# A retention block and a gated feed-forward block on one core: w_out rounded behind the silus, the left-out tokens loaded later, and k of three pairs put in rows on the chip

## The chip, the cores and the metric

The kernel runs on one core of one Trainium2 chip. The metric is the device time of one execution in microseconds (us). Each kernel is run several times and the median is taken.

## The reference

Retention: q, k and v have the shape (8, 8, 576, 64), that is batch, heads, tokens, head size. For each head the scores q k^T / 8 are multiplied by gamma^(i-j) for j <= i and by 0 otherwise, and the result by v. The heads are laid side by side into x of 4608 tokens by 512. Feed-forward, with w_gate and w_val (512 x 1536) and w_out (1536 x 512):

```
g = x @ w_gate
silu = g * (1.0 / (1.0 + np.exp(-g)))
val = x @ w_val
return (silu * val @ w_out)
```

All of it is float32.

## The kernel before, in words

**Tiles and stages.** Heads are taken in pairs: pair i is batch i // 4 and heads 2 (i % 4) and 2 (i % 4) + 1; HP is 4, so pairs 0 to 3 are batch 0, and there are 32. The feed-forward works on tiles of tokens: a first one of 512 (stage 0) and four of 1024 (stages 1 to 4). Stages 1 to 4 use fast matrix products with fewer multiplications, whose sums of operands are made by VectorE and POOL and partly kept in DRAM. Stage 0 is done plainly: `up0(f)` (L859) for the twelve column blocks f of 128 multiplies the tile by w_gate into one PSUM bank and by w_val into a second (banks A and B for even f, C and E for odd f), then ScalarE takes the silu of the first into `io` (L874) and VectorE multiplies it with the second (L875). `down0(f)` (L880) multiplies by w_out, over all four banks.

**Rounding.** All weights are rounded before use. They lie in 18 pieces (six of w_gate, six of w_val, six of w_out, each for two blocks f), loaded in the sequence `order` (L361); "position" below is a place in it, and positions 7, 10, 13, 15, 16 and 17 are w_out. Each piece has two halves, j = 2 x position and the next. `split(j)` (L389) is two ScalarE operations (L398, L399) that write one of two slots (j % 2); `rounding(j)` (L408) is two VectorE operations (L415, L416) that read the slot, and then it emits split(j + 1). When the second half of a piece has been split, its raw place is free and a later position is loaded into it by `load_w` (L368): from position 5 on by POOL's queue (L379, L381).

**Retention.** `load(i)` (L255) issues a pair's transfers on SP's queue: for the pairs from 4 on kn and v by tokens (L290), and q and k "by columns" into `qk` (L299), 32 x 18 x 32 elements in each of 4 + 4 DMAs, so that every piece of memory read is 32 floats. VectorE then turns q and k into rows of the head size by its 32 x 32 block transposes (L477, inside `transposes`, L455), into qT and kT. kT exists once. `tick(t)` (L787) runs one step of a pipeline over pairs: PE does the values of pair t-2, the states and scores of pair t-1; then a list of pieces follows on ScalarE and VectorE: the copy of the even states (L569), the scaling of kn by ScalarE (`keys`, L492), the outputs of pair t-2 (L614), masks and states of pair t-1 (L565 to L593), and the transposes of pair t.

**The left-out tokens.** Pairs 0 to 3 leave out their last 64 tokens at first. `end_loads` (L668) loads q, k and v of these with 20 small DMAs on POOL's queue; `end_transposes`, `end_scores`, `end_masks`, `end_own`, `end_earlier` and `end_to_x` (L680 to L711) compute them inside ticks HP + 1 to HP + 3. Their tiles lie in `spare`, in the part of `rest` that later holds rounded w_out.

**The order.** Every engine runs its instructions in the order in which the program emits them. For stage 0 this is the list `plan` (L1521 to L1546): for f from 2 to 11, the roundings up to a position (`round_until`), `up0(f)`, loads, and ticks 4 to 9 behind f = 2 (ahead of up0(3)), 3, 5, 7, 10 and 11. After the plan come `down0` with the sums of w_out (POOL and VectorE, L904, stored by SP, L974), and ticks 10 to 13.

Of the kernel before, what the change touches and what calls it, by code (L numbers as in the profile page):

```python
# [132 lines left out]
def kernel(  # L133
# [32 lines left out]
    nc = tc.nc  # L166

    B, H, S, D = q.shape
# [3 lines left out]
    HP = H // 2  # L172
    L = D
    NC = S // L
    NFULL = S // P
    CW = NFULL * P
    SQ = 32
# [66 lines left out]
    def whole(i):  # L244

        return HP <= i < needed(2) - 2

    def scaled(i):

        return 0 < i < HP  # L250
# [4 lines left out]
    def load(i):  # L255
# [27 lines left out]
        else:  # L283
# [11 lines left out]
            if not whole(i):  # L295
                queue.dma_start(out=t[:, CW : CW + D], in_=v[b, 2 * p : 2 * p + 2, CW:S, :])
            for n, src in enumerate((q, k)):
                for a in range(P // SQ):
                    queue.dma_start(  # L299
                        out=qk[a * SQ : (a + 1) * SQ, n],  # L300
                        in_=src[b, 2 * p + a // 2, :, (a % 2) * SQ : (a % 2 + 1) * SQ].rearrange("(j t) d -> t j d", t=SQ))
# [121 lines left out]
    for m in range(2):  # L423
# [9 lines left out]
             spare[:, CW : CW + NC * D].rearrange("p (c d) -> p c d", d=D))  # L433
    end_states = spare[:, 3136:3392].rearrange("p (n d) -> p n d", d=D)
    end_raw = spare[:, 1536:2048].rearrange("p (n x) -> p n x", n=2)
    end_q, end_k, end_v = [spare[:, 2048 + 256 * n : 2304 + 256 * n].rearrange("p (n d) -> p n d", d=L) for n in range(3)]
    end_at = [o.rearrange("p (n i) -> p n i", i=L) for o in (outer[:, 0, 384:512], outer[:, 1, 256:384])]
# [17 lines left out]
    def transposes(i):  # L455
# [12 lines left out]
        else:  # L468
            if light(i):
# [5 lines left out]
                pieces.append(scale_q)  # L475
            for n, t in enumerate((qT, kT)):
                pieces.append(lambda n=n, t=t: nc.vector.transpose(out=t, in_=qk[:, n].rearrange("p j d -> p (j d)")))  # L477

# [308 lines left out]
    def tick(t, lo=HP, hi=NP, spread=False, then=None):  # L787
        go_on(len(pieces))
        if lo <= t - 2 < hi:
            own_values(t - 2)  # L790
            if t == HP + 3:
                st[t - 2]["own"] = end_own(1)
        if lo <= t - 1 < hi:
            new_states(t - 1)
        if lo <= t - 2 < hi:
            earlier_values(t - 2)
            if t == HP + 3:
                end_own(0)
                end_earlier()
        if lo <= t - 1 < hi:  # L800
            scores(t - 1, t - 2 < lo)
            if t == HP + 2:
                end_scores()
# [18 lines left out]
        else:  # L822
            pieces.extend(new)
            pieces.extend([then] if then else [])
        if t == HP + 2:
            pieces.append(end_masks)
        if t == HP + 3:
            pieces.append(end_to_x)
# [673 lines left out]
    nc.gpsimd.tensor_copy(out=last_near, in_=near[:, even_heads])  # L1502
    end_loads()
    FIRST = needed(1) - 2
# [9 lines left out]
    def round_until(i):  # L1514
        while todo and order.index(i) >= todo[0]:
            m = todo.pop(0)
            plan.extend(lambda j=j: rounding(j, j != 2 * len(order) - 3) for j in (2 * m, 2 * m + 1))
# [3 lines left out]
    for f in range(2, NF):  # L1521
        if f == 3:
            plan.append(lambda: tick(HP, HP, FIRST))
        round_until({4: 12, 6: 13, 8: 14, 9: 15, 10: 16, 11: 17}.get(f, f + 2))
        last_half = plan.pop() if f + 1 == NF else None
        plan.append(lambda f=f: up0(f, range(HP)))
        if last_half:
            plan.append(last_half)
        if f + 2 == NF:
            plan.append(lambda: split(2 * len(order) - 2))  # L1530
        if f + 1 == NF:
            plan.append(lambda: pool_places.extend(wide_places))
            plan.append(negate)
        if f - 1 in tick_at and f < 7:
            plan.append(lambda t=tick_at[f - 1]: next_load(t))
        if f in tick_at and f > 2:
            plan.append(lambda t=tick_at[f]: tick(t, HP, FIRST))
            if tick_at[f] == HP + 1:
                plan.append(end_transposes)
# [97 lines left out]
```

## Time and profile before

| | |
|---|---|
| runs | median 1015.77 us of 3 (1014.49 to 1016.64) |
| the profiled execution | 1012.77 us |
| its span, first to last instruction | 1011.0 us |
| granted clock of TensorE | 1.000 |
| DMA, mean over the span | 192 GB/s, 273932 packets, 212328 of them under 512 B |
| SP's queue (q1) | 249448 packets, 99.49 MB, 40.5% of 16 engines' span |
| POOL's queue (q0) | 4176 packets, 14.03 MB, 4.2% |

A profile row of a group or of the timeline names the line, the engine, the operation, what it writes and reads, and the shape; the timeline has the start, the duration, and in brackets how long the engine had stood idle before it and what released it. PE is TensorE (PEld its weight loads), DVE VectorE, ACT ScalarE, POOL GpSimd, SP SyncE. "issue" is time in which an engine waited for nothing that the profile shows. Busy shares are means over stages with different limits, so a change in stage 0 is read from the timelines there.

Busy us of the engines in stage 0 and around it, with the mean busy share of the DMA engines:

| stretch, us | PE | VectorE | ScalarE | POOL | DMA |
|---|---|---|---|---|---|
| 40 to 60 | 20.00 | 12.79 | 11.62 | 10.51 | 1.13 |
| 60 to 80 | 19.48 | 14.04 | 9.39 | 2.22 | 1.05 |
| 80 to 100 | 20.00 | 16.05 | 9.87 | 2.17 | 1.09 |
| 100 to 120 | 18.70 | 18.49 | 16.59 | 3.73 | 0.93 |
| 120 to 140 | 20.00 | 18.41 | 5.60 | 8.93 | 0.96 |

### The profile page before, as it was taken

Reading aid. Unit: us, or ns where it says so; the run is one execution under the profiler, and the core shown is the slowest. Engines: PE = TensorE matmul, PEld = TensorE weight load, DVE = VectorE, ACT = ScalarE, POOL = GpSimd, SP = SyncE. Lnnn points to the kernel's source line nnn. Section 1 sums busy time; section 2 is a strip of 40 time slices with the busy share of each in tenths; the row PEclk is TensorE's granted clock in tenths of the full one; section 3 lists DMA queues with packets and bytes.
Section 4 is the critical chain, followed back from the end, with each engine's and each line's share of the span. In section 5 each row is a group of like instructions: output and inputs, shape, how many; then the busy total and the mean of one; then the engine's idle time right before and its main releaser. Section 6 shows DMA issues by size and latency. Waiting matters only on the chain.

```text
span 1011.0 us, 21336 instructions
## 1 busy us (share of the span) xinstructions
PE 1002.8 (99%) x8330; PEld 827.7 (82%) x8330; DVE 717.8 (71%) x1210; ACT 285.7 (28%) x636; POOL 576.3 (57%) x611
## 2 busy tenths in 40 slices
PE   8999999999999999999999999999999999999998
PEld 7645455888888888888888888888888888888887
DVE  5568988678886676977777678866575767566745
ACT  4654622122423321133321202233320012232110
POOL 3511358979587228565565157746672586566614
PEclk9999999999999999999999999999999999999999
DMA  9999977888787886957578786434454454445553
GB/s 228 276 252 281 200 216 260 211 239 217 168 211 235 219 197 218 211 156 198 177 187 222 179 196 202 151 137 155 162 173 141 156 188 146 148 153 185 178 163 103
DMA packets 273932, 194.44 MB, mean 192 GB/s; under 512 B 212328, under 2 KB 241896, under 8 KB 273832
## 3 DMA queue, kind: packets, MB, share of 16 engines
q1 hardware_dynamic: 249448, 99.49, 40.5%
q10 hardware_dynamic: 20208, 79.57, 24.2%
q0 software_dynamic: 4176, 14.03, 4.2%
q8 instruction: 66, 1.08, 0.5%
q14 instruction: 34, 0.28, 0.1%
HBM read 154.11 MB, written 38.93 MB: 191 GB/s over the span
## 4 chain that ended last, share of the span: by engine, by line
PE 91%; SPq 3%; DMA 2%; DVE 1%; issue 1%; ACT 1%; ACTq 0%; DVEq 0%
PE bankB L1208 12%; PE bankE L1208 12%; PE bankA L1208 12%; PE bankC L1208 12%; PE bankE L1415 7%; PE bankC L1415 7%; PE bankB L1415 7%; PE bankA L1415 6%; SPq L299 2%; PE outer L1208 2%; PE inner L1208 2%; PE outer L517 2%; PE outer L544 1%; PE inner L558 1%; PE inner L528 1%
## 5 line engine op out<-in xcount | busy, mean ns | idle before, releaser
L1061 POOL TENSOR_TENSOR rest<-rest 128x512 f32<-128x512 f32 (+1 forms) x143 | 150.7, 1065 | 158.1 <-DVE rest L1061 110.3
L1223 POOL TENSOR_TENSOR arena<-rest,io 128x256 f32<-128x256 f32 x168 | 123.8, 749 | 78.7 <-ACT io L1222 78.1
L1222 ACT ACTIVATE io<-rest 128x256 f32<-128x256 f32 x192 | 79.3, 417 | 209.9 <-DVE rest L1061 139.2
L1208 PE MATMUL bankB<-rest,arena 128*128 128x256 f32 x428 | 110.1, 381 | 0.0
L1208 PE MATMUL bankE<-rest,arena 128*128 128x256 f32 x424 | 107.8, 379 | 0.0
L1061 DVE TENSOR_TENSOR rest<-bankC,rest 128x512 f32<-128x512 f32 x112 | 75.8, 684 | 40.4 <-PE bankC L1208 23.3
L1061 DVE TENSOR_TENSOR rest<-bankB,rest 128x512 f32<-128x512 f32 x110 | 74.8, 685 | 41.5 <-PE bankB L1208 30.4
L1208 PE MATMUL bankA<-rest,arena 128*128 128x256 f32 x408 | 104.0, 379 | 0.0
L1061 DVE TENSOR_TENSOR rest<-bankA,rest 128x512 f32<-128x512 f32 x112 | 75.9, 685 | 38.8 <-PE bankA L1208 20.2
L1061 DVE TENSOR_TENSOR rest<-bankE,rest 128x512 f32<-128x512 f32 x116 | 78.5, 686 | 29.2 <-PE bankE L1208 17.1
L1208 PE MATMUL bankC<-rest,arena 128*128 128x256 f32 x368 | 94.2, 380 | 0.0
L1208 PEld LDWEIGHTS bankB<-rest,arena 128*128 128x128 f32 x428 | 80.7, 190 | 11.9 <-DVE rest L1061 0.9
L1208 PEld LDWEIGHTS bankE<-rest,arena 128*128 128x128 f32 x424 | 80.5, 190 | 11.0
L1208 PEld LDWEIGHTS bankA<-rest,arena 128*128 128x128 f32 x408 | 77.5, 190 | 10.6
L1208 PEld LDWEIGHTS bankC<-rest,arena 128*128 128x128 f32 x368 | 69.4, 190 | 10.0 <-DVE rest L1061 0.6
L1061 POOL TENSOR_TENSOR arena<-arena 128x256 f32<-128x256 f32 (+1 forms) x76 | 70.6, 951 | 8.3 <-PE bankC L1208 7.0
L1415 PE MATMUL bankE<-arena 128*128 128x256 f32 x264 | 61.0, 381 | 0.0
L1415 PE MATMUL bankC<-arena 128*128 128x256 f32 x264 | 60.9, 380 | 0.0
L1415 PEld LDWEIGHTS bankE<-arena 128*128 128x128 f32 x264 | 49.8, 190 | 7.0 <-POOL arena L904 0.2
L1415 PEld LDWEIGHTS bankC<-arena 128*128 128x128 f32 x264 | 49.9, 190 | 6.9
L1415 PE MATMUL bankB<-arena 128*128 128x256 f32 x240 | 55.3, 380 | 0.0
L1415 PE MATMUL bankA<-arena 128*128 128x256 f32 x228 | 52.5, 380 | 0.0
(294 smaller groups left out, 1880.1 us busy)
## 6 DMA issues: line engine op xcount, KB each, us to landing
arena<-up ACTq DMA_DIRECT2D x60, 896.0 KB, 4.8
arena<-dn ACTq DMA_DIRECT2D x60, 384.0 KB, 3.4
arena<-dn SPq DMA_DIRECT2D x44, 384.0 KB, 4.4
out_dram<-rest SPq DMA_DIRECT2D x31, 256.0 KB, 3.5
qk<-in_q_dram SPq DMA_DIRECT2D x108, 72.0 KB, 4.1
qk<-in_k_dram SPq DMA_DIRECT2D x108, 72.0 KB, 3.8
dn<-rest SPq DMA_DIRECT2D x26, 256.0 KB, 3.1
up<-arena SPq DMA_DIRECT2D x13, 512.0 KB, 3.4
```

The source lines that it names most:

```text
L299: queue.dma_start(out=qk[a * SQ : (a + 1) * SQ, n], in_=src[b, 2 * p + a // 2, :, (a % 2) * SQ : (a % 2 + 1) * SQ].rearrange("(j t) d -> t ...
L517: m = nc.tensor.matmul(value(i, hl, c), s["v"][rows, at], ret[rows, c % 2 if whole(i) else hl, c // 2], start=start, stop=start, skip_grou ...
L528: nc.tensor.matmul(z[half[hl], r, c], s["kn"][chunk(i, hl, 2 * c + r)], s["v"][rows, at], start=True, stop=True, skip_group_check=True)
L544: nc.tensor.matmul(xr[half[hl]] if c + 1 == NC else value(i, hl, c), state[half[hl], c, :], s["qT"][half[hl], ts(c, L)], start=False, stop ...
L558: nc.tensor.matmul(sc[chunk(i, hl, 2 * c + r)[0], r if whole(i) else hl, c], kT[half[hl], at], qT[half[hl], at], start=True, stop=True, sk ...
L1061: eng.tensor_tensor(out=out, in0=a, in1=b, op=ALU.add if sign > 0 else ALU.subtract)
L1208: m = nc.tensor.matmul(b[:, g * TB : (g + 1) * TB], w[:, g], x, start=(opens and g == 0), stop=True, skip_group_check=True)
L1222: nc.scalar.activation(out=s, in_=src[:, 0:TB], func=AF.Silu)
L1223: (nc.vector if busy and o != 2 and qd + 1 < NQ else nc.gpsimd).tensor_tensor(out=hid[:, qd, 2 * H + h, 2 * T + t], in0=src[:, TB : 2 * TB ...
L1415: nc.tensor.matmul(b[:, m * TB : (m + 1) * TB], lhs[:, qd, ts(m, P)], w[:, qd], start=(opens and qd == 0 and m == 0), stop=(qd == NQ - 1), ...
```

## The change

Four things change; the arithmetic and the reference's output stay the same.

1. For pairs 5, 6 and 7 (`by_token`) k is not loaded by columns any more. At the start of `transposes`, ahead of `keys`, VectorE transposes kn, which is loaded by tokens anyway, in 32 x 32 blocks into the place of `qk` that k had; 16 ScalarE copies of 32 lanes (`rows_of_k`) then put the blocks in rows in kT, as a piece at the place of the former transpose of k.
2. In the plan, the roundings of w_out (positions 7, 10, 13, 15, 16, 17) are emitted behind `up0(f)` and so behind its silu and product, not ahead of them. Positions of w_gate and w_val stay ahead.
3. `end_loads` is emitted after up0(6) and its roundings (behind the load of position 13 in POOL's queue, ahead of positions 14 to 17) and not ahead of the plan. What is done with the left-out tokens moves by two ticks, to ticks HP + 3 to HP + 5.
4. The tiles of the left-out tokens move from `spare` to the 1536 columns from `sum_at` on, which the first sums of w_out by POOL use later.

```diff
+    def by_token(i):
+
+        return HP < i < needed(1) - 6
...
-            for n, src in enumerate((q, k)):
+            for n, src in enumerate((q,) if by_token(i) else (q, k)):
...
-    end_states = spare[:, 3136:3392].rearrange("p (n d) -> p n d", d=D)
-    end_raw = spare[:, 1536:2048].rearrange("p (n x) -> p n x", n=2)
-    end_q, end_k, end_v = [spare[:, 2048 + 256 * n : 2304 + 256 * n].rearrange("p (n d) -> p n d", d=L) for n in range(3)]
+    ends_at = rest[:, sum_at : sum_at + 1536]
+    end_states = ends_at[:, 1280:1536].rearrange("p (n d) -> p n d", d=D)
+    end_raw = ends_at[:, 0:512].rearrange("p (n x) -> p n x", n=2)
+    end_q, end_k, end_v = [ends_at[:, 512 + 256 * n : 768 + 256 * n].rearrange("p (n d) -> p n d", d=L) for n in range(3)]
...
-            for n, t in enumerate((qT, kT)):
-                pieces.append(lambda n=n, t=t: nc.vector.transpose(out=t, in_=qk[:, n].rearrange("p j d -> p (j d)")))
+            flat = [qk[:, n].rearrange("p j d -> p (j d)") for n in range(2)]
+            pieces.append(lambda: nc.vector.transpose(out=qT, in_=flat[0]))
+
+            def rows_of_k():
+
+                blocks = flat[1].rearrange("p (g n t) -> p g n t", n=2, t=SQ)
+                to = kT.rearrange("p (c w t) -> p c w t", w=2, t=SQ)
+                for r in range(2):
+                    for hl in range(2):
+                        cs = slice((hl + r) % 2, NC, 2)
+                        gs = slice(hl * (NC // 2 + (1 - r)), hl * (NC // 2 + (1 - r)) + len(range(NC)[cs]))
+                        for w in range(2):
+                            for n in range(2):
+                                nc.scalar.copy(out=to[(2 * hl + n) * SQ : (2 * hl + n + 1) * SQ, cs, w],
+                                               in_=blocks[(2 * r + w) * SQ : (2 * r + w + 1) * SQ, gs, n])
+
+            if by_token(i):
+                nc.vector.transpose(out=flat[1], in_=kn)
+                pieces.append(rows_of_k)
+            else:
+                pieces.append(lambda: nc.vector.transpose(out=kT, in_=flat[1]))
...
-            if t == HP + 3:
+            if t == HP + 5:
                 end_own(0)
                 end_earlier()
...
-            if t == HP + 2:
+            if t == HP + 4:
                 end_scores()
...
-        if t == HP + 2:
+        if t == HP + 4:
             pieces.append(end_masks)
-        if t == HP + 3:
+        if t == HP + 5:
             pieces.append(end_to_x)
...
-    end_loads()
...
-        round_until({4: 12, 6: 13, 8: 14, 9: 15, 10: 16, 11: 17}.get(f, f + 2))
-        last_half = plan.pop() if f + 1 == NF else None
+        if f < 10:
+            round_until(f + 2)
         plan.append(lambda f=f: up0(f, range(HP)))
-        if last_half:
-            plan.append(last_half)
+        if f in (4, 6) or f > 7:
+            round_until({4: 12, 6: 13}.get(f, f + 6))
         if f + 2 == NF:
             plan.append(lambda: split(2 * len(order) - 2))
+        if f == 6:
+            plan.append(end_loads)
...
-            if tick_at[f] == HP + 1:
+            if tick_at[f] == HP + 3:
                 plan.append(end_transposes)
```

More of the change, by code (lines that the diff above doesn't have):

```diff
@@ L824, in tick @@
             pieces.extend([then] if then else [])
-        if t == HP + 2:
+        if t == HP + 4:
             pieces.append(end_masks)
-        if t == HP + 3:
+        if t == HP + 5:
             pieces.append(end_to_x)
```

## The prediction

> **What bounds the kernel now.** I read the page first, then PE's waits, then the timelines of PE, ScalarE, VectorE and POOL between 37 and 130 us, where every edit lies.
>
> ```profile
> span 1011.0 us, 21336 instructions
> ...
> PE 1002.8 (99%) x8330; PEld 827.7 (82%) x8330; DVE 717.8 (71%) x1210; ACT 285.7 (28%) x636; POOL 576.3 (57%) x611
> ```
>
> PE is busy for all but 8.2 us of the span. Its waits from 40 us to 1000 us, in one row (engine, line, what it waited for, us in total, times, longest):
>
> ```profile
> PE bankA L871 <- ACT io L874: 1.8, 2, 1.3
> ```
>
> So between the start-up and the last store only two waits stop PE, and both are waits for the silu (L874) that empties a bank two f earlier. PE's timeline has them (start, us, last bracket: idle before, and releaser):
>
> ```profile
> 71.47 3.70 PE L871 MATMUL bankA<-rest,arena 128*128 128x512 f32 x8 [0.52 <-ACT io L874]
> ...
> 103.74 3.70 PE L871 MATMUL bankA<-rest,arena 128*128 128x512 f32 x8 [1.30 <-ACT io L874]
> ```
>
> They are up0(6) and up0(10). All other f take 6.97 us (54.46 to 61.43, 61.43 to 68.39, 71.47 to 78.44): no further wait is hidden in them. Why was silu(8) late? ScalarE before it:
>
> ```profile
> 99.52 0.69 ACT L398 ACTIVATE rest<-rest 128x512 f32<-128x512 f32 x1 [8.51 <-issue]
> ...
> 102.54 0.66 ACT L399 ACTIVATE rest<-rest 128x512 int32<-128x512 uint32 x1
> 103.11 0.58 ACT L874 ACTIVATE io<-bankA 128x512 f32<-128x512 f32 x1
> ```
>
> Bank A was full at 92, but three splits (L398, L399) stand ahead of the silu, and the first had to wait for a slot that VectorE empties. VectorE was late itself, by column loads of k (and, at 59.55, of q):
>
> ```profile
> 59.55 0.78 DVE L477 STREAM_TRANSPOSE qT<-qk 128x576 f32<-128x576 f32 x1 [1.66 <-DMA qk<-in_q_dram]
> 65.36 0.78 DVE L477 STREAM_TRANSPOSE kT<-qk 128x576 f32<-128x576 f32 x1 [5.03 <-DMA qk<-in_k_dram]
> ...
> 97.44 0.78 DVE L477 STREAM_TRANSPOSE kT<-qk 128x576 f32<-128x576 f32 x1 [3.01 <-DMA qk<-in_k_dram]
> ```
>
> The chain is: column load, kT, rounding, split, silu, PE. What the change can win in this execution is 0.52 + 1.30 = 1.82 us, 0.18% of 1015.77 us, because nothing else stops PE there and its matmuls are the same ones after.
>
> **The change, part by part.**
> (1) k by columns goes for pairs 5, 6, 7: 12 DMAs of 72 KB leave SP (52.17, 69.08, 85.50: 5.61 + 2.13 + 4.32 = 12.1 us of its queue). VectorE's waits of 5.03 and 3.01 go with them. VectorE's work is unchanged: three transposes of 128x576 (0.73 to 0.78 each) read kn in place of qk, and stand earlier, behind the product of the odd f. The new wait there is for kn: at tick 5 ScalarE scaled kn at 54.88 without waiting, and the transpose would come at 54.05, so at most 0.8 us, on an engine that then waits for q until 59.55 anyway. Of keys, which must follow the transpose, I expect no more than that.
> (2) ScalarE gets 48 copies of 32 lanes with 128 or 160 elements. No row has this shape. Below: 128x64 from PSUM, L641, 0.11 from start to next start; above: 128x288 SBUF to SBUF, L474, 0.95 for two, so 0.48. Nearest: L611, 64x128, 0.53 for two at 133.23, next start 0.44 on, so 0.22 each. 16 x 0.22 = 3.5 us a pair (1.8 to 7.7). They run behind keys, where ScalarE stood idle from 57 to 67.18 (tick 5) and from 91.0 to 99.52 (tick 7). At tick 6 there is no such gap, and they delay splits 19 to 21 by 3.5.
> (3) Silus ahead of the w_out splits. silu(4) had splits 14, 15 and 16 in front, and keeps 14; silu(8) had 26 to 28 and keeps 26. A split is 1.13, so each is 2 x 1.13 = 2.3 earlier, on top of VectorE's earlier start. silu(4): q at 59.5, transpose 0.7, rounding 12 from 60.3, split 14 to 62, silu done by 62.7; PE wants it at 70.95. Covered by 8 us.
> (4) The left-out tokens. End matmuls move from ticks 6 and 7 to ticks 8 and 9: tick 6 took 2.56 on PE, tick 7 3.04, tick 8 2.26, so 0.30 and 0.78 are moved, sum zero, but up0(10) comes 1.08 earlier still, at 102.45 - 0.52 - 1.08 = 100.85. The 20 loads leave POOL's queue at 37 and stand behind the weight load of position 13 (w_out), ahead of 14 to 17. What they took:
>
> ```profile
> 37.10 3.81 POOL L672 DMA_DIRECT2D rest<-in_q_dram  x7
> 44.05 0.65 POOL L672 DMA_DIRECT2D rest<-in_q_dram  x1 [3.15 <-DMA rest<-in_moe_w_gate_dram]
> 44.69 4.33 POOL L672 DMA_DIRECT2D rest<-in_k_dram  x8
> 49.01 2.42 POOL L677 DMA_DIRECT2D rest<-in_v_dram  x4
> 51.39 0.75 POOL L381 DMA_DIRECT2D rest<-in_moe_w_out_dram  x1
> ```
>
> That is 14.3 us, with a wait for a load that stands eight places ahead on the queue. In the new place: tick 6 ends on PE at 70.65; ScalarE runs even and keys (1.2) from 69.8, copies 3.5, splits 19 and 20 (2.4), silu(6) 0.5, split 21 1.2, so 78.6; position 13 is issued to 79.3, the 20 loads to 93.6. **Position 14, w_val for f 10 and 11, is issued at 93.6 and not at 87.17.** Its load took 9.4 us (the seven gate and w_val loads of this queue 8.7 to 9.7): 102.3 to 103.0 (103.3). Split 1.25 and the second half of the rounding 0.75 make the weights ready at 104.3 to 105.0. PE wants them for bank B of up0(10) at 100.85 + 3.43 = 104.3. I take half, 0.35 us of a new wait.
> The transposes of these tokens (k issued by 79.3 + 11.9 = 91.2, with 3.7 to 4.6 to land as it had there) end near 96.5 on VectorE; silu(8) follows 2.4 later at 98.9, wanted at 100.85: covered by 2 us.
> (5) end_masks is now the last of tick 8 on VectorE and end_own the second of tick 9 on PE (117.5 + 0.28 = 117.8). In the old order tick 8's last transpose ended at 119.27, because even waited behind a split for w_out of position 17 (issued 105.13, landed 113.6). Masks end 6.0 after that landing. Position 17 follows split 29, which follows position 14: 102.6 + 2.4 = 105.0; at the 5.9 of position 16 it lands at 110.9 and the masks are 0.9 early, at 8.4 they are 1.6 late. With SP's load of pair 9 over by then (it starts when pair 7's rows are copied, 93, not 108) I take 5.9 and no cost.
> (6) end_raw and the rest lie where the first output sums of POOL go (L904 at 108.14), so POOL starts them after tick 9, near 120.5. It did its second only at 119.06 and then stood 9.03 us for stores from 127.7, which SP began at 132.01 behind loads. SP is 12 us earlier: nothing.
>
> Sum: -1.82 + 0.35 = -1.5. The profiled execution's 1012.77 (span 1011.0 and 1.77 around it) becomes 1011.3; it lies 3.00 under the median of the runs, and I apply the difference there: 1015.77 - 1.5 = **1014.3**.
>
> **The rivals.**
> A, the wait is only exchanged: position 14 or 17 lands at the late end of its rows (9.4 to 9.7; 8.4), PE stands 0.7 to 1.6 at up0(10) or in tick 9. For it: DMA share is 0.95 to 1.16 from 85 to 100. Against: 12 loads fewer. 1014.7 to 1015.6, no change. 0.18.
> B, slower: POOL's 20 issues stretch beside the rounding, which now runs there. At the longest weight issue against the shortest (0.98 to 0.70, factor 1.4) 11.2 us of issues become 15.7; with position 9 landing late (2.3 us on split 18) position 14 is issued at 100.4, its weights come at 111.8, and PE stands 7.5: 1015.77 - 1.8 + 7.5 = 1021.5. It decides from an issue of position 14 at about 96.8 on (1.8 won, 2.0 more for the bound). Against: eight issues at 44.69 took 549 to 552 ns, beside rounding until 45.4. 0.14. The Trainium skill, page "SBUF — State Buffer", section "SBUF: two separate sides", states such a rule: while VectorE runs a two-port operation, GpSimd cannot write the descriptors of its DMAs. By that rule this rival would hold; the 549 to 552 ns speak against it here, though on few instructions.
> C, more than the profile has: the runs' median is 3.00 above the profiled execution. Were half of it waits of the same chain, 1.5 more would go: 1012.8, all of it 1011.3. For it: column loads took 2.8 to 11.1 us to land, so the chain can vary. Against: the profile shows nothing of it. 0.18.
> D, copies at 0.48: 4.2 us more at tick 6, which delays positions 13 and 14 by as much; 2.7 slower than before, 1018.5; at half of that, no change. 0.05.
>
> **How the numbers follow.** Forecast 0.45. A measurement can tell about 0.2%, 2.0 us: faster ends at 1013.7. The runs before spread over 2.15 us, so a third of the forecast (0.15) falls below that line, and 0.30 above. Faster 0.15 + 0.18 (C) = 0.33; same 0.30 + 0.18 (A) + 0.02 (D) = 0.50; slower 0.14 (B) + 0.03 (D) = 0.17. The range takes the forecast, A and the near half of C, and leaves out B, the slow part of D and the far end of C: 1011.6 to 1017.0.
>
> **What would show it.** PE's row of waits for L874 gone between 60 and 110; no VectorE wait for in_k columns before tick 8; position 14 issued near 94 and no PE wait on its weights over 0.7; masks ahead of end_own; POOL's issues still 0.55. The prediction is wrong if up0(10) or tick 9 shows a wait over 1.8, if a ScalarE copy takes 0.4, or if the time moves by more than 1.9 with PE's waits as forecast.

## The result and the profile after

After: median 1020.13 us of 5 runs (1018.75 to 1021.29); before, beside it on the same chip, 1015.48 of 5 (1014.49 to 1016.64). The ratio is 1.0047, with a 95% interval from 1.0024 to 1.0070: slower by 4.65 us. The forecast was 1014.3, its range ended at 1017.0. The profiled execution took 1020.75 us with a span of 1018.8.

PE's timeline of after has both waits of before changed. The wait at up0(6) is gone. In their place PE stops three times (start, us, and in the last bracket the idle time and its releaser; L895 is up0, L541 the values in a tick):

```profile
104.80 3.70 PE L895 MATMUL bankA<-rest,arena 128*128 128x512 f32 x8 [3.25 <-ACT io L898]
110.20 3.70 PE L895 MATMUL bankB<-rest,arena 128*128 128x512 f32 x8 [1.71 <-DVE arena L420]
...
124.87 0.46 PE L541 MATMUL outer<-ret,v 64*64 64x64 f32 x16 [1.41 <-DVE rest L717]
```

The first two are up0(10), its gate bank and its second bank; the third is tick 9, which waits for the masks of the left-out tokens. 3.25 + 1.71 + 1.41 = 6.37, against 0.52 + 1.30 = 1.82 in before: 4.55 more, which is the size of the loss in the medians. The two profiled executions themselves lie 7.98 us apart (1020.75 and 1012.77): 4.9 of it in stage 0, 2.3 behind it and 0.7 ahead of it. A second profile of before (below) shows that its own waits differ between executions, so the agreement of 4.55 with 4.65 is partly luck.

What made the first two begins on POOL; where the third comes from is worked out at step 5 below. POOL's timeline from position 13's load to position 14's (L385 and L383 are weights, L696 and L701 the tokens):

```profile
84.94 0.70 POOL L385 DMA_DIRECT2D rest<-in_moe_w_out_dram  x1 [1.99 <-ACT rest L403]
85.64 3.87 POOL L696 DMA_DIRECT2D rest<-in_q_dram  x7
94.50 0.55 POOL L696 DMA_DIRECT2D rest<-in_q_dram  x1 [4.98 <-DMA rest<-in_moe_w_out_dram]
95.03 4.33 POOL L696 DMA_DIRECT2D rest<-in_k_dram  x8
99.36 2.40 POOL L701 DMA_DIRECT2D rest<-in_v_dram  x4
101.72 0.80 POOL L383 DMA_DIRECT2D rest<-in_moe_w_val_dram  x1
```

The form is that of before, 4.33 us for eight issues included. But the eighth token load waits 4.98 us (3.15 in before) for the weight load eight places ahead, and position 14 is issued at 101.72 (the prediction had 93.6). The same two loads, positions 13 and 14, in before's POOL timeline:

```profile
84.39 0.70 POOL L381 DMA_DIRECT2D rest<-in_moe_w_out_dram  x1 [6.66 <-ACT rest L399]
87.17 0.76 POOL L379 DMA_DIRECT2D rest<-in_moe_w_val_dram  x1 [2.07 <-ACT rest L399]
```

Position 13 is issued as late as in before (84.94 against 84.39); the 20 loads behind it put position 14 back by 14.55 us.

ScalarE's timeline shows both ends of the chain, the copies (L494) and what waits (L402 is the first half of a split, L898 the silu):

```profile
56.45 5.11 ACT L494 COPY kT<-qk 32x160 f32<-32x160 f32 x16
...
71.52 0.67 ACT L402 ACTIVATE rest<-rest 128x512 f32<-128x512 f32 x1 [3.19 <-DMA rest<-in_moe_w_gate_dram]
...
102.86 0.67 ACT L402 ACTIVATE rest<-rest 128x512 f32<-128x512 f32 x1 [3.72 <-issue]
...
104.16 0.58 ACT L898 ACTIVATE io<-bankA 128x512 f32<-128x512 f32 x1
...
108.20 0.66 ACT L402 ACTIVATE rest<-rest 128x512 f32<-128x512 f32 x1 [2.32 <-DMA rest<-in_moe_w_val_dram]
```

A copy takes 5.11 / 16 = 0.32 us. The split at 102.86, ahead of silu(8), waits for VectorE; the one at 108.20 waits for position 14's load, 6.5 us after its issue. What held VectorE are the transposes of the tokens:

```profile
97.89 0.45 DVE L706 STREAM_TRANSPOSE rest<-rest 128x256 f32<-128x256 f32 x1 [1.18 <-DMA rest<-in_q_dram]
101.92 0.45 DVE L706 STREAM_TRANSPOSE rest<-rest 128x256 f32<-128x256 f32 x1 [3.58 <-DMA rest<-in_v_dram]
```

The second one reads k, whose eight loads POOL issued until 99.36. The row names a load of v, the last of its queue; in the kernel the instruction reads only k.

### The profile page after: what moved, and what is told of

It is laid out like the page before. It is cut to its first block, busy times and chain, and to the rows that moved or that the text cites. A ratio compares the mean times of both kernels' runs of the same rounds, so it can differ in the third digit from the quotient of the medians.

```text
span 1018.8 us, 21372 instructions
## 1 busy us (share of the span) xinstructions
PE 1005.5 (99%) x8330; PEld 828.2 (81%) x8330; DVE 718.8 (71%) x1210; ACT 300.5 (29%) x684; POOL 576.4 (57%) x611
## 4 chain that ended last, share of the span: by engine, by line
PE 85%; DMA 3%; POOL 2%; issue 1%; DVE 1%; SPq 1%; ACT 0%; DVEq 0%; ACTq 0%; POOLq 0%
PE bankB L1232 12%; PE bankE L1232 11%; PE bankA L1232 11%; PE bankC L1232 11%; PE bankE L1439 7%; PE bankC L1439 7%; PE bankB L1439 7%; PE bankA L1439 6%; PE inner L1232 2%; PE outer L1232 2%; PE outer L541 2%; DMA rest<-in_moe_w_out_dram 2%; PE outer L568 1%; PE inner L582 1%; PE inner L552 1%; PE bankA L906 1%
```

## The experiments

In all tables "stage 0" is the time from the start of up0(2) to the first down product in the profiled execution, and the waits are those of PE between them. Part 2 is the silus ahead of the w_out roundings, part 1 is k by tokens, parts 3 and 4 are the late loads with their tiles. Each ratio is the one on record, taken against runs of before on the same chip; it is not the quotient of the two medians. A kernel that starts from after is compared with after by these ratios.

### The parts one by one and in pairs

Parts were undone in the changed kernel. Part 1 undone loads k by columns for every pair:

```diff
-        return HP < i < needed(1) - 6
+        return False
```

Part 2 undone has the plan of before:

```diff
-        if f < 10:
-            round_until(f + 2)
+        round_until({4: 12, 6: 13, 8: 14, 9: 15, 10: 16, 11: 17}.get(f, f + 2))
+        last_half = plan.pop() if f + 1 == NF else None
         plan.append(lambda f=f: up0(f, range(HP)))
-        if f in (4, 6) or f > 7:
-            round_until({4: 12, 6: 13}.get(f, f + 6))
+        if last_half:
+            plan.append(last_half)
```

Parts 3 and 4 undone have the loads ahead of the plan, the work on the tokens in ticks HP + 1 to HP + 3 and the tiles in `spare` (of this edit only the plan is shown):

```diff
+    end_loads()
...
-        if f == 6:
-            plan.append(end_loads)
...
-            if tick_at[f] == HP + 3:
+            if tick_at[f] == HP + 1:
                 plan.append(end_transposes)
```

| parts in the kernel | median us | ratio to before, 95% | stage 0 | PE's waits in stage 0 |
|---|---|---|---|---|
| none (before) | 1014.14 | 1.0008 [0.9992, 1.0024] | 86.46 | up0(6) 1.67, up0(10) 1.91 |
| 2 | 1014.36 | 0.9997 [0.9982, 1.0012] | 81.11 | tick 10 1.07 |
| 1 | 1016.58 | 1.0016 [0.9996, 1.0036] | 81.70 | tick 10 1.57 |
| 1, 2 | 1017.45 | 1.0025 [1.0006, 1.0043] | 82.60 | tick 9 1.49, tick 10 0.35 + 1.58 |
| 3, 4 | 1023.19 | 1.0084 [1.0062, 1.0106] | 90.32 | up0(10) 6.63 |
| 2, 3, 4 | 1021.04 | 1.0062 [1.0040, 1.0085] | 88.80 | up0(10) 1.10 + 3.94, tick 9 0.83 |
| 1, 3, 4 | 1024.21 | 1.0104 [1.0083, 1.0125] | 91.10 | up0(10) 8.53 |
| all (after) | 1020.13 | 1.0047 [1.0024, 1.0070] | 87.87 | up0(10) 3.25 + 1.71, tick 9 1.41 |

The row of before is its second profile; the first one, ahead of the prediction, has a stage 0 of 83.01 with waits of 0.52 and 1.30.

**The late loads are enough for a loss.** The four kernels without them lie within 0.25% of before, the four with them 0.47 to 1.04% over it; alone they cost 0.84%. In three of the four pairs with and without them the intervals are apart. In the fourth they overlap: parts 1 and 2 alone are at 1.0025, all four at 1.0047. Part 2 makes good some of the loss: 1.0104 becomes 1.0047, with the intervals apart; 1.0084 becomes 1.0062, with intervals that overlap. PE's wait in the kernel with parts 3 and 4 alone:

```profile
107.42 6.27 PE L895 MATMUL bankA<-rest,arena 128*128 128x512 f32 x8 [6.63 <-ACT io L898]
```

Before as a kernel of its own. Expected:

> The kernel before, unchanged, profiled a second time beside its own timed runs. It settles how much of a difference of 1 to 3 us between two profiled executions is only the execution. In the one profile so far, the stretch from the start of stage 1 to the last instruction took 838.2 us; in after and four variants 839.4 to 840.9. If that rest is chance of the execution, this profile shows 839 to 841 too, with one or two stops of PE called issue near 276, and a span of 1012 to 1014. If the changes cost something behind stage 0, it shows 838.2 and no such stop. Both expect the waits of 0.52 and 1.30 us for the silus again, and a time ratio of 1.000 within 0.002.

The first branch held for that stretch: from stage 1 to the end it took 1016.6 - 176.45 = 840.2 us, as in the variants, with a stop of 1.00 at 277, so it is no cost of the change. The span was 1016.6 and not 1012 to 1014, because the silu waits are larger in this execution, as its PE timeline shows:

```profile
72.85 3.70 PE L871 MATMUL bankA<-rest,arena 128*128 128x512 f32 x8 [1.67 <-ACT io L874]
105.73 5.40 PE L871 MATMUL bankA<-rest,arena 128*128 128x512 f32 x8 [1.91 <-ACT io L874]
```

Behind the second one PE's granted clock is lower. The rows of the windows give the stretch, its length, PE's busy time and instructions, the granted clock, the DMA share and GB/s:

```profile
105.00:110.00 5.00, 4.27 (x7) 0.69 0.97 263
110.00:115.00 5.00, 5.00 (x43) 0.97 1.16 314
```

1.67 + 1.91 + (5.40 - 3.70) = 5.28 us against 1.82 in the other profile. One profile is one draw: this execution took 1018.36 us, the first one 1012.77, and the median lies between. Of the 5.6 us between the two, 3.5 are in stage 0 and 2.0 behind it.

Part 2 alone:

> The kernel before with part 2 alone: w_out rounded behind the silus. Both theories: silu(8) has one split ahead of it and not three, so it is done 2.3 us earlier than at 103.69, silu(4) likewise; PE's waits of 0.52 and 1.30 go: 1.5 to 2.0 us under the kernel before. If the time stays, those waits were no more than the profiled execution's own.

Missed. Both waits went, PE began the down products 2.00 us earlier (120.39 against 122.39), and the time did not move: PE stopped 1.07 at tick 10.

Part 1 alone:

> The kernel before with part 1 alone: k of pairs 5 to 7 in rows by VectorE's blocks and ScalarE's copies; loads of the left-out tokens and roundings of w_out as before. ScalarE gets 48 copies of 0.32 (5.1 us a pair, as measured in after, not 3.5). Theory (the copies put 5.1 us ahead of the splits at tick 6, and the column loads' lateness at tick 7 is gone; the two about cancel): silu(8) is up to 1.5 earlier or later than in before, its wait 0 to 3 us; time within 1.5 of before. Rival (part 1 alone does what it is for: VectorE is ahead, splits and silus follow): both waits of before gone, time 1.5 to 3 under before. Second rival (the copies alone are a loss): wait for silu(8) above 3, time 2 or more over before.

The rival's mechanism held in the trace (both waits under 0.2), its time did not: 1.57 at tick 10, ratio 1.0016.

Parts 1 and 2, tokens early:

> The changed kernel with parts 3 and 4 undone: the left-out tokens load ahead of the plan and are worked on in ticks 5 to 7, in their old place; silus first and k by tokens stay. Theory (the 20 late loads on POOL's queue cost the time, by three waits of PE of 3.25, 1.71 and 1.41 us): all three go, and the two old ones of 1.82 as well, so 1.0 to 2.0 us under the kernel before. Rival 1 (the 48 ScalarE copies cost it, 5.1 us a pair): still 3 to 5 us over the kernel before. Rival 2 (the loss lies behind stage 0): also still over it, with no wait of PE between 60 and 130 us.

Missed, by about 4 us by the ratio: new waits at ticks 9 and 10 came in place of the others, with a granted clock of 0.67 behind the last (130 to 135). So parts 1 and 2 together cost something without the late loads; what makes these waits was not followed up.

Parts 3 and 4 alone:

> The kernel before with the later loads of the left-out tokens alone (parts 3 and 4 of the change); k of pairs 5 to 7 by columns again, w_out roundings ahead of the products again. Theory (three losses that do not need each other; the late loads on POOL are the largest): the weights of position 14 come late for up0(10) again, 2 to 5 us over before, and as the splits stand ahead of the silu again, the wait for silu(8) is 3 or more. Time 1.5 to 4 us over before. Rival (the loss needs the combination: without the copies and with the roundings in their old places, the loads find room): within 1 us of before. A wait of tick 9 for the masks is expected under 0.5 by the theory, since without part 2 the last splits are not moved.

The direction held, the size was twice what was expected: one wait of 6.63, and a lower clock behind it. The split ahead of silu(8) waited 3.91 us for position 14's load, which was issued at 98.00.

Without part 1:

> The changed kernel with part 1 undone: k of the three pairs by columns again, no copies on ScalarE; silus first and late tokens stay. Theory: the late loads alone still make VectorE and position 14 late, but they start up to 8 us earlier without the copies at ticks 5 and 6, so one or two of the three waits stay, smaller: 0 to 3 us over the kernel before. Rival 1: without the copies the loss is gone, 1 to 2 us under the kernel before.

The copies are not needed for the loss: position 13 is issued as late without them (85.42, up0(2) being 0.56 later in this profile). The size was missed: about 6 us over before where 0 to 3 were expected, and the three waits, 5.87 in all, are hardly smaller than in after.

Without part 2:

> The changed kernel without part 2: w_out rounded ahead of the products as in before, with k by tokens and the late loads kept. Theory (late loads hold up0(10), and without part 2 the silus wait behind more splits): waits at up0(10) of 5 to 7 in one, and then a lower granted clock for about 5 us; no wait over 0.5 at tick 9, since PE comes there later; time 1 to 3 over after, like the late loads alone (1.0084). Rival (part 2 is what costs the 1.41 at tick 9, and the rest is as in after): 5 at up0(10), none at tick 9, time 1 to 1.5 under after.

One wait, as the theory had it, but of 8.53, and nearer 6 than 3 us over after by the ratios.

### Where the late loads hold PE

Each of these starts from the changed kernel.

The 20 loads on SP's queue:

```diff
-                    nc.gpsimd.dma_start(
+                    nc.sync.dma_start(
...
-                nc.gpsimd.dma_start(out=end_v[half[hl ^ x], 2 * x : 2 * x + 2],
+                nc.sync.dma_start(out=end_v[half[hl ^ x], 2 * x : 2 * x + 2],
```

> The changed kernel with the 20 loads of the left-out tokens issued on SP's queue, at the same place of the program, so that positions 14 to 17 have POOL's queue to themselves. Theory: position 14 is issued when its split frees the place (near 87), the wait of 1.71 goes, and the loads land ahead of 97 as SP stands idle from 74 to 80, so that of 3.25 goes or shrinks: 1 us over to 2 us under the kernel before. Rival 1: the copies stay, so does the loss: 3 to 5 us over.

1018.25 us, ratio 1.0041 [1.0022, 1.0060]. Position 14 was issued at 87.06 and both waits at up0(10) went, as the theory had it, but the masks in tick 9 took their place:

```profile
121.05 0.46 PE L541 MATMUL outer<-ret,v 64*64 64x64 f32 x16 [3.63 <-DVE rest L717]
```

So the time missed, and lies where the rival had it. The rival's cause is another: the last kernel of this section keeps the copies and has no loss.

Position 14's load ahead of the 20 (`end_loads` behind f == 7):

```diff
-        if f == 6:
+        if f == 7:
             plan.append(end_loads)
```

> The changed kernel with one thing moved: POOL issues the weight load of position 14 ahead of the 20 loads of left-out tokens, which follow it directly. Every other instruction and its order is as in after. Theory (up0(10) stood 3.25 and 1.71 us because position 14's load stood behind those 20 on the queue): position 14 is issued 10 to 16 us earlier, near 86 to 92, its weights are ready before 103, and bank B's wait of 1.71 goes; the wait of 3.25 for silu(8) falls as far as splits waited for that load; it stays as far as VectorE waits for the transposes of the tokens themselves (their loads land no earlier, 101.9), 1 to 3 us. Tick 9 keeps 1.4 or more. Time 1 to 3 us under after, still over before. Rival (the wait is for ScalarE's copies or for the rows of k by tokens, not for the queue): up0(10) waits as in after, 4.5 to 5 in all, time within 0.7 of after.

1021.81 us, ratio 1.0085 [1.0066, 1.0104]: the theory fell. The wait for bank B went, and the one for silu(8) grew to 5.61, because the tokens' loads now came later still and VectorE stood at their transposes. PE's timeline of this kernel:

```profile
106.56 6.63 PE L895 MATMUL bankA<-rest,arena 128*128 128x512 f32 x8 [5.61 <-ACT io L898]
```

And VectorE's, with the second transpose of the tokens (101.92 in after):

```profile
103.61 0.45 DVE L706 STREAM_TRANSPOSE rest<-rest 128x256 f32<-128x256 f32 x1 [3.87 <-DMA rest<-in_v_dram]
```

So two waits stand side by side at up0(10). Next, the transposes moved instead, behind the roundings of f 8:

```diff
+        if f == 8:
+            plan.append(end_transposes)
...
-            if tick_at[f] == HP + 3:
-                plan.append(end_transposes)
```

> The changed kernel with one thing moved: VectorE's two transposes of the left-out tokens stand behind the roundings of f 8, no longer behind tick 7. In after, VectorE waited 1.18 and 3.58 us there for the tokens' loads (the second transpose at 101.92), and split, silu(8) and up0(10) behind it. Theory (two waits stand side by side at up0(10): the transposes, which hold silu(8) to 104.16, and position 14, whose weights are ready only near 110.2): the wait for silu(8), 3.25 in after, falls under 0.5, but PE then waits as much more for the weights of bank B: 1.71 becomes 4 to 5.5. Sum at up0(10) 4.3 to 5.5, against 4.96 in after; time within 1 us of after. Rival 1 (the transposes alone carry the loss): both waits shrink, sum under 2.5, time 2.5 to 4 us under after. Rival 2 (silu(8) waits for a split of position 13 whose load is late): the wait for silu(8) stays above 2.

1020.86 us, 1.0060 [1.0039, 1.0081]. Nearly as expected (5.95 in all, where up to 5.5 was): silu(8) is in time, and PE, in this kernel's timeline, waits as much longer for position 14.

```profile
101.45 3.70 PE L895 MATMUL bankA<-rest,arena 128*128 128x512 f32 x8 [0.52 <-ACT io L898]
110.58 5.49 PE L895 MATMUL bankB<-rest,arena 128*128 128x512 f32 x8 [5.43 <-DVE arena L420]
```

Both moved (the two edits above together):

> The changed kernel with both moved: the load of position 14 ahead of the 20 loads, as in the run with that alone, and the two transposes of the tokens behind the roundings of f 8. Theory (each of the two alone makes PE wait about 5 us at up0(10); only without both does it go): the wait at up0(10) falls under 1 us in all, and what is late next is tick 9 or tick 10, as with the loads on SP's queue: 1.5 to 3.6 us for the masks or for z. Time 1 to 3 us under after, 1.5 to 4 over before. Rival (the copies of k are what makes silu(8) late): up0(10) still waits 2 or more, time within 1 us of after.

1020.38 us, 1.0061 [1.0039, 1.0082]. The time missed: 1 to 3 us under after were expected, and it is no lower. Up0(10) waits 1.54 in place of 4.96 (under 1 was expected), and tick 9 takes the rest, since positions 15 to 17 are issued from 103.80 on and VectorE rounds position 16 ahead of the masks. PE's timeline:

```profile
105.71 3.70 PE L895 MATMUL bankB<-rest,arena 128*128 128x512 f32 x8 [1.54 <-DVE arena L420]
122.74 0.71 PE L541 MATMUL outer<-ret,v 64*64 64x64 f32 x16 [3.77 <-DVE rest L717]
```

Both moved, and positions 16 and 17 rounded behind ticks 8 and 9:

```diff
-        if f in (4, 6) or f > 7:
+        if f in (4, 6, 8, 9):
             round_until({4: 12, 6: 13}.get(f, f + 6))
-        if f + 2 == NF:
-            plan.append(lambda: split(2 * len(order) - 2))
...
             plan.append(lambda t=tick_at[f]: tick(t, HP, FIRST))
+            if f > 9:
+                round_until(f + 6)
+            if f + 2 == NF:
+                plan.append(lambda: split(2 * len(order) - 2))
```

> The changed kernel with all that the 20 loads hold moved out of their way: position 14 ahead of them on POOL, the tokens' transposes behind the roundings of f 8, w_out positions 16 and 17 rounded behind ticks 8 and 9. The loads themselves stay late on POOL's queue. Theory (all three waits of the changed kernel have this one cause): no wait at up0(10) over 1.6, the wait at tick 9 falls from 1.4 to 3.8 to under 0.5, stage 0 is 3 to 5 shorter than in after; time 3 to 6 us under after, about that of before or 1 to 2 under it. Rival 1 (positions 15 to 17, issued behind the loads near 104, are late for the down products too): PE waits 2 or more for w_out at the first down products, time within 2 of after. Rival 2 (the masks are late by the end scores themselves): tick 9 waits 2 or more as before.

1018.60 us, 1.0043 [1.0028, 1.0058]: missed, since it can't be told from after's 1.0047. Three waits stayed, 0.28 and 2.42 at up0(10) and 2.09 at tick 9. The 2.42 is for position 14, whose rounding stands behind the tokens' transposes on VectorE; the second of these waited 1.15 for k and began at 105.61. The 2.09 comes from a split of position 15 (issued at 105.30, behind the 20 loads), which waited 6.40 ahead of silu(9).

The same order of the last roundings with the 20 loads on SP, the transposes and position 14 in the places of after:

> The changed kernel with the 20 loads issued by SP's queue instead of POOL's, and w_out's positions 16 and 17 rounded behind ticks 8 and 9 (the loads' move alone left one wait, 3.63 us for the masks in tick 9). Theory (the loads on POOL make the waits at up0(10); the masks are late because VectorE's list of tick 8 stands behind the rounding of position 16, whose load lands late): no wait over 0.5 at up0(10), under 1 at tick 9, none at tick 10; down products begin 81 to 82 us after up0(2) (after: 87.9), time 5 to 7 us under after, within 1 of before or up to 2 under it. Rival (the masks are late in their own place, from end scores that PE makes in tick 8): tick 9 keeps 2 or more; time as with the move to SP alone, 1.004 of before.

1013.91 us, 1.0001 [0.9981, 1.0020]. The loss is gone, so POOL's queue and the place of the last roundings made it between them: with the queue alone relieved it stayed, and it stayed with the last roundings later and the loads on POOL, there in other places (1.0043). The last roundings later with all else as in after was not run. PE's timeline still has small waits:

```profile
104.53 3.70 PE L895 MATMUL bankB<-rest,arena 128*128 128x512 f32 x8 [0.42 <-DVE arena L420]
118.99 0.46 PE L541 MATMUL outer<-ret,v 64*64 64x64 f32 x16 [1.20 <-DVE rest L717]
```

The masks keep 1.20 us where under 1 was expected. VectorE's list of tick 8 begins there behind the product of silu(10), and silu(10) behind a split that waited 2.41 us for position 16's load; moving that was not tried.

### Why the two silu waits gave nothing back

These start from before. First the silus ahead at f 4, 6 and 8 alone, w_out's positions 15 to 17 rounded as in before:

```diff
-        round_until({4: 12, 6: 13, 8: 14, 9: 15, 10: 16, 11: 17}.get(f, f + 2))
+        round_until({9: 15, 10: 16, 11: 17}.get(f, f + 2))
         last_half = plan.pop() if f + 1 == NF else None
         plan.append(lambda f=f: up0(f, range(HP)))
+        if f in (4, 6, 8):
+            round_until({4: 12, 6: 13, 8: 14}[f])
```

> The kernel before with the silus first at f 4, 6 and 8 alone (w_out positions 12 to 14 behind the product); the last three w_out positions (15 to 17) are rounded ahead of up0(9) to up0(11) as before. Theory (silus first takes the two waits away, and the new wait at tick 10 of the run with all six comes from the last w_out roundings, which there stand between up0(11) and tick 9's list on VectorE): the waits of 0.52 and 1.30 go, no wait over 0.3 at tick 10, the down products start 1.5 to 2.0 earlier than in before, time 1.0 to 2.0 us under before, ratio 0.998 to 0.999. Rival 1 (the wait at tick 10 comes only because PE is 2 us earlier there, whatever VectorE does): a wait of 0.7 to 1.5 in tick 10 stays, time within 0.7 of before. Rival 2 (silu(8) still has a w_out split ahead of it that matters): the wait of 1.30 stays at over 0.5.

1013.28 us, 0.9999 [0.9984, 1.0013]: rival 1. PE is 2 us earlier and stands at tick 10, as its timeline shows:

```profile
130.43 0.69 PE L528 MATMUL inner<-v,kn 64*64 64x64 f32 x32 [1.57 <-issue]
```

VectorE's roundings of position 17 (L415, L416), which stand ahead of its list of tick 9, are long in the same kernel:

```profile
120.07 1.34 DVE L415 TENSOR_SCALAR rest<-rest 128x512 int32<-128x512 int32 x1
121.44 1.64 DVE L416 CUSTOM_DVE_ANT_0 rest<-rest 128x1024 uint16<-128x1024 uint16 x1
```

The profile says "issue", but L528 writes the bank `inner`, and VectorE's last read of it (L593) ended at 130.33. **The same pair of rows in before holds the answer.** VectorE's last read there:

```profile
129.07 0.47 DVE L593 SCALAR_TENSOR_TENSOR state<-state,tab,inner 128x256 f32<-128x256 f32 x1
```

PE's next write to the bank:

```profile
129.74 0.65 PE L528 MATMUL inner<-v,kn 64*64 64x64 f32 x32
```

VectorE was done at 129.54 and PE came at 129.74. Of the 1.82 us, at most 0.20 could be had before PE met VectorE, and VectorE itself did not come earlier: its last read ended 90.16 us after the start of up0(2) in before and 89.98 after it here. In the second profile of before the same slack is larger, 1.25 us (132.17 and 133.42), beside 5.28 us of silu waits.

POOL's first sums later (on top of the edit before this one):

```diff
-            plan.append(negate)
...
+        if m == 1:
+            negate()
+            groups.pop(0)()
-        if groups:
+        if groups and m:
             groups.pop(0)()
```

> The kernel before with the silus first at f 4, 6 and 8 (as in the run of that alone, whose time was that of before) and POOL's first output sums released later: ScalarE's two negated copies of w_out and the first group of sums stand behind tick 10. In the run without this, VectorE's last two roundings ran beside POOL's sums and took 1.34 + 1.64 and 0.89 + 1.63 us, where others take 0.42 + 0.69, and PE waited 1.57 at tick 10 for what VectorE does behind them. Theory (VectorE beside POOL is the wait at tick 10): the last four roundings' parts take 0.42 to 0.45 and 0.69, VectorE's tick 9 ends about 3 us earlier, the wait at tick 10 is under 0.3, and the down products start no later; time 1 to 2 us under before, ratio 0.998 to 0.999. Rival 1 (the roundings are long by themselves): they stay at 1.3 and 1.6, the wait stays, ratio 1.000. Rival 2 (POOL's sums are needed where they were): stage 0 is 1.5 shorter, but POOL's sums or SP's stores are late behind it, and stage 1 or the end gives it back; ratio 1.000 or over.

1016.30 us, 1.0018 [1.0002, 1.0034]. The roundings fell to 0.39 and 0.69 and tick 10's wait went, as the theory had it; but rival 2 took the gain back with waits at ticks 12 and 13, at a POOL sum in stage 1, and 1.43 near 276. VectorE's timeline, with a rounding of position 17:

```profile
118.23 0.39 DVE L415 TENSOR_SCALAR rest<-rest 128x512 int32<-128x512 int32 x1
118.65 0.69 DVE L416 CUSTOM_DVE_ANT_0 rest<-rest 128x1024 uint16<-128x1024 uint16 x1
```

PE's timeline, with what came instead:

```profile
152.53 0.27 PE L552 MATMUL outer<-qT,kT 64*64 64x64 f32 x2 [0.72 <-DVE kT L477]
162.16 0.69 PE L544 MATMUL outer<-qT,state 64*64 64x64 f32 x32 [0.72 <-DVE state L593]
...
221.31 1.13 PE L1208 MATMUL bankB<-rest,arena 128*128 128x256 f32 x4 [0.92 <-POOL arena L1061]
```

w_out's position 17 rounded behind tick 9 instead, POOL's sums left where they were:

```diff
-        round_until({9: 15, 10: 16, 11: 17}.get(f, f + 2))
-        last_half = plan.pop() if f + 1 == NF else None
+        if f + 1 < NF:
+            round_until({9: 15, 10: 16}.get(f, f + 2))
...
             plan.append(lambda t=tick_at[f]: tick(t, HP, FIRST))
+            if f + 1 == NF:
+                round_until(17)
```

> The kernel before with the silus first at f 4, 6 and 8, and the two roundings of w_out's last position (17, needed only by the fifth down product) put behind tick 9 on VectorE and ScalarE. Theory (the silu waits were hidden behind a second chain of nearly equal length: w_out position 17, its roundings beside POOL's sums, VectorE's tick 9, PE's tick 10; in before PE came there only 0.20 us after VectorE): no wait at up0(6), up0(10) or tick 10, the down products start about 81 us after up0(2) (before: 83.0 in one profile, 86.5 in the other), and the time is 2 to 4 us under before, ratio 0.996 to 0.998. Rival 1 (a third chain of the same length stands behind, at ticks 11 to 13 or in POOL's sums): stage 0 shorter by under 1, ratio 0.999 to 1.001. Rival 2 (the roundings are late for the fifth down product): a wait of 0.5 to 3 on position 17's weights there, ratio about 1.000.

1014.30 us, 1.0005 [0.9987, 1.0022]. Tick 10 does not wait any more, but in the profiled execution up0(6) does, 0.69 and 0.64 (its second bank's weights), and stage 0 took 82.51. No gain can be told. Why up0(6) waited there and not with the edit of f 4, 6 and 8 alone stays open; the order up to it is the same in both, so it may be the execution.

The same with part 1:

> As e15_last_later, and part 1 of the change with it (k of pairs 5 to 7 by VectorE's blocks and ScalarE's copies). Theory (with the silus first and tick 10 free, part 1 takes nothing off PE's path; its copies, 5.1 us a pair, delay the loads of later positions by that): no wait over 0.5 more than in e15_last_later, time within 1 of it. Rival 1 (SP's queue, 12 loads shorter, lets later pairs come earlier): 1 to 2 under it. Rival 2 (the copies delay positions 13 to 17 so that ticks 8 to 10 wait, as in the run with tokens early, where it was 3.4 in all): 2 to 3 over it.

1015.59 us, 1.0017 [1.0004, 1.0030]: a wait of 1.88 at up0(11), with a lower clock behind it, in place of the others. Neither kernel nor any variant is faster than before by more than its interval.

## Why the prediction was wrong

**Step 1 (k by columns) was right for VectorE**: its waits of 5.03 and 3.01 went. The wait for the new transpose fell on ScalarE's keys instead, 1.18 at ticks 6 and 7, where at most 0.8 was allowed.

**Step 2 (copies) was mis-sized, and put in the wrong place.** 0.32 us each and not 0.22; 5.1 a pair, inside the bounds of 1.8 to 7.7. The prediction let them run in ScalarE's idle time from 57 at tick 5. But the split that stood at 55.74 in before follows keys, so it follows the copies too: it began at 61.59, position 9's load went out at 63.12 and not at 57.26, and split 18 waited 3.19 for it at 71.52.

**Step 3 (silus first) did what it says, and the gain was not there.** The prediction counted 1.82 us because no other wait was hidden in up0's periods. It did not ask where PE's next hand-over from VectorE stands: at tick 10, 0.20 us behind. Part 2 alone is at 0.9997.

**Step 4 (the late loads) failed most, on the issue of position 14: 93.6 forecast, 101.72 measured.** Of the 8.1 us, 6.3 are position 13's (84.94 against 78.6: 3.3 from the even copy at 73.13 behind split 18, 1.2 from keys, 1.6 from the copies, the rest small) and 1.8 the queue's wait of 4.98 where 3.15 had been taken from before. So the forecast counted on part 1 to bring position 13 forward by 5.8 us (78.6 against 84.39 in before), and it came no earlier at all; that position 9 lands late on split 18 stood in rival B alone. One term erred the other way: position 14's load was split 6.5 us after its issue, not 9.4. The weights were ready at 110.2, not at 104.3 to 105.0. The transposes of the tokens were forecast to end near 96.5, with a cover of 2 us for silu(8); they ended at 102.4. The forecast loss of 0.35 was 4.96.

**Step 5 (masks cost nothing) failed**, and not by the term that it watched. Position 17 was issued at 110.84, not at 105.0, but it did not hold the masks: the even copy behind its split ended at 119.04, and VectorE's first step behind it began at 120.29 without waiting. VectorE's list of tick 8 came late by position 16. The split for its load (issued at 106.18, in before at 102.36) stands ahead of silu(10); the product and the roundings of position 16 follow, and then the list, whose last piece are the masks (L717). The rows of ScalarE and of VectorE in after:

```profile
114.22 0.69 ACT L402 ACTIVATE rest<-rest 128x512 f32<-128x512 f32 x1 [0.60 <-DMA rest<-in_moe_w_out_dram]
...
116.02 0.69 DVE L899 TENSOR_TENSOR arena<-bankB,io 128x512 f32<-128x512 f32 x1 [0.59 <-ACT io L898]
...
124.37 0.45 DVE L717 TENSOR_TENSOR rest<-outer,near 128x128 f32<-128x128 f32 x2
```

VectorE has no idle time between the last two. That the 1.41 us are near the bound of 1.6 given there is chance: the bound was worked out for another landing, and PE came to tick 9 some 6 us later than forecast.

**Step 6** held: POOL started its sums at 127.33 and not near 120.5, but the time behind stage 0 is 840.5 us in after, against 838.2 and 840.2 in the two profiles of before. The kernel with POOL's sums later shows that they can cost time there: moved by some 14 us (119.85 to 134.48), they go with 842.0 us against 838.3.

**The rivals.** A had the places (up0(10) and tick 9), at 0.7 to 1.6 instead of 6.37 together. B had the size (1021.5) and an issue of position 14 behind its point of 96.8, at 101.72, but its mechanism is wrong: the first seven issues, beside VectorE's roundings (which ran to 89.03), took 3.87 us, against 3.81 in before; the eight of 4.33 stood beside no rounding. With both moved, eight issues stood partly beside roundings and took 4.39. The time went into waits for earlier loads. The rule by which VectorE keeps GpSimd from its descriptors, weighed there, finds no support in these rows. C took the gap between the profiled execution and the median for waits that can be won. That the gap is partly such waits is supported by the second profile (5.28 us); that taking them away gives time is not (0.9997, 0.9999). D's larger copies came true by half, 0.32 between 0.22 and 0.48; the kernel without them (1.0062) is no faster than after (1.0047).

The bound of 0.2% was too fine: before alone took 1010.66 to 1018.51 us on one chip, and its two profiled executions differ by 3.5 us in stage 0 alone.

## What to carry to other kernels

A wait that is taken away was worth no more here than the slack at the next hand-over to that engine. That slack is the time from the end of the instruction that releases to the start of the one that would wait; measure it in the trace of before for each hand-over that follows. Work that is put into a queue ahead of other loads delays all of these, and where they feed several consumers, moving one consumer out of the way only shows the wait of the next: silu(8), position 14's weights and the masks took turns here. Ask of each inserted group which instruction now stands behind it, not whether the engine has idle time nearby.

## What the runs showed of the hardware

**A stop of PE can cost more than its length.** Eight matmuls of up0 take 3.60 to 3.70 us; behind waits of 1.88, 1.91, 3.94, 5.43, 5.61, 6.63 and 8.53 us they took 5.40, 5.40, 5.13, 5.49, 6.63, 6.27 and 5.14, up to 2.9 more, at a granted clock down to 0.57. A row of the windows of parts 3 and 4 alone:

```profile
105.00:110.00 5.00, 2.58 (x3) 0.58 1.06 385
```

Behind 3.25 us in after, and behind 2.42 with both moved and the last roundings later, they took 3.70. The Trainium skill, page "TensorE: Matmul & The Clock Gate", section "Part 1: The HAM clock gate", has a window of some 3.4 us that runs freely, and halves the clock after an idle one. The traces do not agree: the stops of 1.88 and 1.91 us are shorter than such a window and were followed by a lower clock. What decides it is not shown here.

**VectorE beside POOL.** The second half of a rounding, which reads two tiles in SBUF, took 1.64 us beside POOL's sums and 0.69 without them; the first half, which reads one, 1.34 against 0.39. The Trainium skill, page "SBUF — State Buffer", section "SBUF: two separate sides", says that such a VectorE operation and a GpSimd operation that reads SBUF shut each other out; the kernels with POOL's sums early and later agree for the second half. For operations that read one tile the section has a lock in a two-port mode only, and no run here shows the mode of the first half.

**POOL's queue held eight loads at a time.** With one weight load ahead the eighth token load waited for it (4.98 us); with two ahead (position 14 moved) the seventh waited 1.87 and the eighth 3.80.
